# Linear attention and a SiLU layer on one core: second-product blocks between a batch's attention steps, a merged kv product, and a new order of loads

## The chip, the cores and the metric

The kernel runs on 1 core of one Trainium2 chip. The metric is the device time of one execution in microseconds. A profile is one further execution, recorded instruction by instruction; its span runs from the first to the last instruction, and its own time is a little longer than the span. The engines are TensorE (PE, its weight loads PEld), VectorE (DVE), ScalarE (ACT), GpSimd (POOL), and SyncE (SP), which only issues transfers.

## What is computed

Batch 8, 8 heads, 576 positions, 64 channels per head; the layer behind it maps 512 to 2048 to 512. Weights and data arrive and leave in float32.

```python
q_s = exp(q - max(q, -1)); q_s /= sum(q_s, -1)        # over the channels of a head
k_s = exp(k - max(k, 2));  k_s /= sum(k_s, 2)         # over the positions
kv  = einsum('bhsd,bhse->bhde', k_s, v)
x   = einsum('bhsd,bhde->bhse', q_s, kv)              # then (4608 tokens, 512)
h   = x @ w_in                                        # first product, 512 -> 2048
out = (h * sigmoid(h)) @ w_out                        # second product, 2048 -> 512
```

## The kernel before

**Attention of a batch.** q, k and v come in two head groups (`cc` 0 and 1), each a tile of 128 partitions by 1152 numbers. ScalarE takes the exponentials (`exp_q` L105, `exp_k` L108). `qsum` (L115) sums q over its channels on VectorE and takes the reciprocal, `qnorm` (L122) multiplies by it, mostly on GpSimd. The normalised q is transposed to `qT`: on TensorE for the first two batches (`tr` L140, copied from PSUM by `trcopy` L149), by a transposing DMA for the others (`q_transpose` L134). `vcast` (L110) casts v into `vaug`, which has a column of constants behind each head, so that `kv` (L153) gives the sum for k's normalisation along with the product. `kv` accumulates in PSUM banks 6 and 7; `kvcopy` (L165) divides by that column and writes `kvn`. `xt_mm` (L186) then multiplies `kvn` and `qT`, and `xt_evac` (L196) casts the result to `XTS`, the transposed input of the layer; `xt` (L200) does both for a head group, always through banks 6 and 7.

**The layer.** The 4608 tokens go in chunks of 512 (`NCH` is 9). Chunk 0 is special: its first product is done for the whole batch 0, 576 tokens wide, in 16 "wide" units of 8 matmuls (`wide_mm` L217, `wide_silu` L228), which rotate through three pairs of banks, 0 to 5. Chunk 1 then has only its remaining 448 tokens to do (`mm1` L252, banks 0 and 1 in turn). A unit's h goes through a tanh on ScalarE (L212) and one multiply on VectorE (L213) into `GTS`. Chunk 0's second product is a plain one, 16 blocks of four matmuls over all 512 outputs (`mm2_plain` L267), which accumulate in banks 2 to 5; `mm2_plain_out` (L277) scales them into output tiles and stores them. From chunk 1 on the second product goes by Strassen's seven products (`prod` L316, two halves each), with differences of weights T1 to T4 (`t_op` L306; T3 is written into part of W2 itself) and of activations (`s_op` L296), all on VectorE.

**The order** is written out by hand. Each engine runs its instructions in the order in which the program emits them. After the start-up, which is listed line by line, a list `units` holds the blocks for TensorE: 16 wide units (0 to 15); then, from `b1 = begin[1]` = 16 on, 32 units with chunk 1's first product and chunk 0's plain second product in turn; then 30 units for each later chunk. `plan(u, f)` puts a step in front of unit `u`: all steps planned for `u` are emitted, in the order in which they were planned, and then the unit. The steps for batch 1 lie in front of the wide units, those for batch 2 among chunk 1's units, those for batch t + 1 in chunk t.

**Loads.** Batch 0 comes over SP's queue; W1 (`load_w1`, with a cast to bfloat16), W2 (`load_w2`, to float16) and batches 1 and 2 over GpSimd's queue, where an issue stands in line with GpSimd's computing; batches from 3 on over SP's. Each of the tiles `qt`, `kt` and `vt` has three buffers, one and a half batches. `heat` (L400) runs matmuls on a constant tile into bank 5.

Of the kernel before, what the change touches and what calls it, by code (L numbers as in the profile page):

```python
# [17 lines left out]
def kernel(  # L18
# [96 lines left out]
    def qsum(b, cc):  # L115
        if "zq" not in st[b]:
            st[b]["zq"] = ap.tile([128, 2, J, 2], FP32, name="zq", bufs=2)
            st[b]["rzq"] = ap.tile([128, 2, J, 2], FP32, name="rzq", bufs=2)
        nc.vector.reduce_sum(out=st[b]["zq"][:, cc], in_=half(st[b]["eq"], cc), axis=AX.X)  # L119
        nc.vector.reciprocal(out=st[b]["rzq"][:, cc], in_=st[b]["zq"][:, cc])  # L120
# [44 lines left out]
    def kvcopy(b, cc):  # L165
        kp = PS[:, 6:8, cc * 128:cc * 128 + E1]
        rz = ap.tile([128, 2], FP32, name="rz", bufs=2)
        nc.vector.reciprocal(out=rz, in_=kp[:, :, D])
        nc.vector.tensor_tensor(
            out=kvn[b % 3][:, cc],  # L170
            in0=kp[:, :, 0:D],
            in1=rz[:, :, None].to_broadcast([128, 2, D]),
            op=ALU.mult,
        )
# [102 lines left out]
    def mm2_plain_out(t):  # L277
        for i, m in enumerate((1, 2, 3, 0)):
            o = mp.tile([128, DM], FP32, name="op", bufs=2)
            if i % 2 == 0:  # L280
                nc.scalar.activation(out=o, in_=PS[:, 2 + m], func=ACT.Copy, scale=OS)
            else:
                nc.vector.tensor_scalar_mul(out=o, in0=PS[:, 2 + m], scalar1=OS)  # L283
# [132 lines left out]
    heat(18)  # L416
# [4 lines left out]
    vcast(0, 0, nc.gpsimd, 1, 2)  # L421
# [28 lines left out]
    trcopy(0, 1, 5, J, 3)  # L450
# [12 lines left out]
    wide_mm(1, (0, 1), (0,))  # L463
# [4 lines left out]
    wide_mm(1, (0, 1), (1,))  # L468
# [36 lines left out]
    def first(part):  # L505
        for n in range(2):
            if part == 0:
                mm1_mm(1, FB[n], n, (0, 1))
            else:
                mm1_mm(1, FB[n], n, (2, 3))  # L510
                mm1_silu(1, FB[n], n)
# [64 lines left out]
    plan(b1 + 10, lambda: t_op(2, nc.vector, 0, 4))
# [9 lines left out]
    for i, x in enumerate((29, 31)):  # L586
        plan(b1 + x, lambda i=i: xt(2, i))
# [63 lines left out]
```

## Time and profile before

| | |
|---|---|
| three runs | 294.33, 297.22, 297.41 us; median 297.22 |
| profiled execution | 296.02 us, span 294.2 us |
| mean granted TensorE clock | 0.98 |
| busy, PE / PEld / DVE / ACT / POOL | 268.8 / 169.9 / 200.9 / 156.6 / 71.1 us |
| moved by DMA | 45.85 MB, 156 GB/s over the span |

Line numbers (L213) are those of the kernel before. In rows of the order of time stand start, length, engine, line, operation, out<-in with shapes, number of instructions, and in square brackets how long the engine was idle just before and what released it. In rows of waits stand the waiting engine and line, what it waited for, the total in us, how often, and the longest. In rows of DMA issues stand the queue, the number, the size as it arrives, and the time from issue to landing. A busy PE is not a PE at its peak: the granted clock tells how fast it was let run.

### The profile page before, as it was taken

How to read it: one execution, taken by the hardware profiler on the slowest of the kernel's cores; microseconds unless marked ns; L12 is line 12 of the kernel's file. 1: busy time of each engine (PE TensorE's matmuls, PEld its weight loads, DVE VectorE, ACT ScalarE, POOL GpSimd, SP SyncE). 2: the span in 40 equal slices, each digit the busy share in tenths (PEclk: the TensorE clock that was granted, in tenths of full speed). 3: DMA queues.
4: the chain of work that ended last, by engine and by line, in shares of the span. 5: the costliest groups of instructions: out<-in, count | busy, mean ns of one | idle time of the engine just before them, and what ended most of it. 6: DMA issues, size and time to landing. Idle time of an engine off the chain costs nothing.

```text
span 294.2 us, 5752 instructions
## 1 busy us (share of the span) xinstructions
PE 268.8 (91%) x2339; PEld 169.9 (58%) x2372; DVE 200.9 (68%) x287; ACT 156.6 (53%) x236; POOL 71.1 (24%) x58
## 2 busy tenths in 40 slices
PE   8696969997699999999999999999999999999980
PEld 3354734443356666665665666566666666666860
DVE  3748554796299749975995699579947755775810
ACT  5747562563466468545856584667464446445120
POOL 1964832081018001800460064007200000000000
PEclk9999798999979999999999999999999999999998
DMA  7899999119877638664864678350324004200506
GB/s 256 262 250 274 311 234 376 59 40 331 264 204 196 237 74 240 166 230 106 276 166 165 145 238 244 101 125 14 68 48 98 2 0 88 57 0 18 128 0 143
DMA packets 36074, 45.85 MB, mean 156 GB/s; under 512 B 16080, under 2 KB 20688, under 8 KB 36048
## 3 DMA queue, kind: packets, MB, share of 16 engines
q1 hardware_dynamic: 29568, 34.22, 41.2%
q0 software_dynamic: 6480, 11.27, 15.2%
q8 instruction: 18, 0.29, 0.4%
q14 instruction: 8, 0.07, 0.1%
HBM read 36.70 MB, written 9.44 MB: 157 GB/s over the span
## 4 chain that ended last, share of the span: by engine, by line
PE 76%; DVE 11%; ACT 4%; DMA 3%; issue 2%; POOL 1%; SPq 1%; DVEq 0%; ACTq 0%; POOLq 0%
PE PS L240 33%; PE PS L328 31%; PE PS L220 4%; DVE GT L213 3%; DMA vt<-in_v_dram 3%; PE PS L269 2%; DVE S L304 2%; DVE zq L119 2%; PE PS L157 2%; PE PS L190 2%; ACT XT L86 1%; ACT sg L212 1%; DVE T L314 1%; DMA out_dram<-op 1%; PE PS L402 1%
## 5 line engine op out<-in xcount | busy, mean ns | idle before, releaser
L212 ACT ACTIVATE sg<-PS 128x512 f32<-128x512 f32 (+2 forms) x144 | 85.5, 598 | 99.5 <-PE PS L240 89.3
L213 DVE SCALAR_TENSOR_TENSOR GT<-sg,PS 128x512 f16<-128x512 f32 (+2 forms) x144 | 96.5, 679 | 61.0 <-ACT sg L212 60.5
L240 PE MATMUL PS<-XT,W 128*128 128x512 bf16 (+1 forms) x480 | 126.3, 381 | 5.1 <-DVE op L283 3.2
L240 PEld LDWEIGHTS <-W 128*128 128x128 bf16 x512 | 49.5, 99 | 43.7 <-issue 6.2
L125 POOL TENSOR_TENSOR eq<-eq,rzq 128x1152 bf16<-128x1152 bf16 x15 | 31.6, 2116 | 126.5 <-ACT sg L212 83.1
L328 PEld LDWEIGHTS <-S 128*128 128x128 f16 x512 | 49.6, 98 | 18.4 <-issue 2.1
L328 PEld LDWEIGHTS <-GT 128*128 128x128 f16 x384 | 37.5, 99 | 14.6 <-issue 2.6
L328 PE MATMUL PS<-W,S 128*128 128x256 f16 x256 | 32.9, 273 | 0.8 <-ACT sb L344 0.7
L328 PE MATMUL PS<-W,GT 128*128 128x256 f16 x256 | 33.3, 276 | 0.1
L328 PE MATMUL PS<-T,S 128*128 128x256 f16 x256 | 32.7, 273 | 0.0
L304 DVE TENSOR_TENSOR S<-GT 128x2048 f16<-128x2048 f16 x16 | 25.2, 1574 | 0.0
L119 DVE TENSOR_REDUCE zq<-eq 128x18 f32<-128x1152 bf16 x16 | 21.5, 1345 | 4.2 <-ACT eq L105 4.2
L88 POOL CAST vaug<-vt 128x1152 bf16<-128x1152 f32 (+1 forms) x15 | 22.7, 1536 | 0.8 <-DMA vt<-in_v_dram 0.8
L105 ACT ACTIVATE eq<-qt 128x1152 bf16<-128x1152 f32 x16 | 18.6, 1162 | 2.4 <-DMA qt<-in_q_dram 2.4
L108 ACT ACTIVATE ek<-kt 128x1152 bf16<-128x1152 f32 x16 | 18.6, 1163 | 1.4 <-DMA kt<-in_k_dram 1.4
L220 PE MATMUL PS<-XT,W 128*128 128x288 bf16 x128 | 18.5, 299 | 0.6 <-ACT XT L86 0.3
L86 ACT CAST XT<-PS 128x1024 bf16<-128x1024 f32 (+2 forms) x17 | 16.4, 964 | 5.0 <-PE PS L190 5.0
L328 PE MATMUL PS<-T,GT 128*128 128x256 f16 x128 | 16.5, 273 | 0.7 <-ACT sc L344 0.7
L269 PE MATMUL PS<-W,GT 128*128 128x512 f16 x64 | 16.3, 379 | 0.0
L220 PEld LDWEIGHTS <-W 128*128 128x128 bf16 x128 | 12.7, 102 | 5.4 <-issue 1.0
L304 DVE TENSOR_TENSOR S<-GT,S 128x2048 f16<-128x2048 f16 x8 | 13.7, 1718 | 0.0
L402 PE MATMUL PS<-warm 128*128 128x512 bf16 x31 | 9.6, 466 | 2.0 <-DVE warm L387 1.2
(48 smaller groups left out, 138.6 us busy)
## 6 DMA issues: line engine op xcount, KB each, us to landing
out_dram<-ow SPq DMA_DIRECT2D x64, 128.0 KB, 2.4
qt<-in_q_dram SPq DMA_DIRECT2D x12, 576.0 KB, 4.9
kt<-in_k_dram SPq DMA_DIRECT2D x12, 576.0 KB, 6.4
vt<-in_v_dram SPq DMA_DIRECT2D x12, 576.0 KB, 7.5
qt<-in_q_dram POOLq DMA_DIRECT2D x4, 576.0 KB, 8.7
kt<-in_k_dram POOLq DMA_DIRECT2D x4, 576.0 KB, 9.4
vt<-in_v_dram POOLq DMA_DIRECT2D x4, 576.0 KB, 11.6
W<-in_moe_w_out_dram POOLq DMA_DIRECT2D x4, 512.0 KB, 14.1
```

Of the source, the lines that this page charges most:

```text
L86: eng.copy(out=o, in_=i)
L88: eng.tensor_copy(o, i)
L105: nc.scalar.activation(out=half(st[b]["eq"], cc), in_=jgd(b, "qt", cc), func=ACT.Exp)
L119: nc.vector.reduce_sum(out=st[b]["zq"][:, cc], in_=half(st[b]["eq"], cc), axis=AX.X)
L125: eng.tensor_tensor(out=e, in0=e, in1=r[:, :, :, None].to_broadcast([128, J, 2, D]), op=ALU.mult)
L212: nc.scalar.activation(out=s, in_=i, func=ACT.Tanh, scale=OS)
L213: nc.vector.scalar_tensor_tensor(out=o, in0=s, scalar=1.0, in1=i, op0=ALU.add, op1=ALU.mult)
L220: nc.tensor.matmul(out=PS[:, 2 * (fb % 3) + n, 0:S // 2], lhsT=W1[:, c, fb * 128:(fb + 1) * 128], rhs=XTS[0][:, c, n * (S // 2):(n + 1) * ...
L240: nc.tensor.matmul(out=PS[:, bank, o0:TCH], lhsT=W1[:, c, fb * 128:(fb + 1) * 128], rhs=XTS[t % 2][:, c, o0:TCH], start=(c == 0), stop=(c ...
L269: nc.tensor.matmul(out=PS[:, 2 + tb, :], lhsT=GTS[t % 2][:, fc, tb * 128:(tb + 1) * 128], rhs=W2[:, fc, :], start=(fc == 0), stop=(fc == N ...
L304: eng.tensor_tensor(out=SS[i - 1], in0=in0, in1=in1, op=op)
L328: nc.tensor.matmul(out=PS[:, WBANK[i], m * HN:(m + 1) * HN], lhsT=a[:, fc, m * 128:(m + 1) * 128], rhs=bb[:, fc, :], start=(first and m == ...
```

## The change

- Chunk 1's 32 units are reordered. Before, two units of its first product came first, then two blocks of the second, then the two in turn, with batch 1's last kv and X products all ahead of the first unit. Now four blocks of chunk 0's second product come first, batch 1's cast of v, kv products and the two X products are planned in front of the second, third and fourth of them, and three units of chunk 1's first product are left for the end.
- `kv_both` runs the kv products of both head groups and one `kvcopy`; it takes the place of two separate steps for batches 1 to 7 (batch 0 keeps two).
- `qsum` can do one head of a group at a time, so that the two halves are planned in front of different units (batches 1 and 2).
- `mm2_plain_out` writes into the wide tiles `ow` (three buffers, shared with the later chunks) in place of its own tile `op` (two buffers).
- In the start-up, GpSimd no longer casts v before it issues W1; ScalarE does; the second head group's casts of v and kv product are moved ahead of the first matmuls with W1, and the warming matmuls change in number and once in bank.
- W2's first quarter is issued ahead of batch 1's v; the other parts, and batch 2's loads, at other places of GpSimd's order; batch 3's loads four units earlier.
- The steps of batches 1 and 2 and the T differences are planned in front of other units.

```diff
-    def qsum(b, cc):
+    def qsum(b, cc, gs=None):
...
+        z, e = st[b]["zq"][:, cc], half(st[b]["eq"], cc)
+        if gs is None:
+            nc.vector.reduce_sum(out=z, in_=e, axis=AX.X)
+        else:
+            nc.vector.reduce_sum(out=z[:, :, gs], in_=e[:, :, gs, :], axis=AX.X)
+        if gs != 0:
+            nc.vector.reciprocal(out=st[b]["rzq"][:, cc], in_=z)
...
-    def kvcopy(b, cc):
...
+    def kvcopy(b, c0=0, c1=2):
+        kp = PS[:, 6:8, 0:256].rearrange("p r (c x) -> p r c x", x=128)[:, :, c0:c1, 0:E1]
+        rz = ap.tile([128, 2, 2], FP32, name="rz", bufs=2)[:, :, 0:c1 - c0]
+        nc.vector.reciprocal(out=rz, in_=kp[:, :, :, D])
+        for c in range(c0, c1):
+            nc.vector.tensor_tensor(
+                out=kvn[b % 3][:, c],
...
+    def kv_both(b):
+        kv(b, 0)
+        kv(b, 1)
+        kvcopy(b)
...
     def mm2_plain_out(t):
-        for i, m in enumerate((1, 2, 3, 0)):
-            o = mp.tile([128, DM], FP32, name="op", bufs=2)
...
+        for ms in ((1, 2), (3, 0)):
+            ow = mp.tile([128, 2, DM], FP32, name="ow", bufs=3)
+            for i, m in enumerate(ms):
+                if i == 0:
+                    nc.scalar.activation(out=ow[:, i], in_=PS[:, 2 + m], func=ACT.Copy, scale=OS)
+                else:
+                    nc.vector.tensor_scalar_mul(out=ow[:, i], in0=PS[:, 2 + m], scalar1=OS)
+                store(t, m * 128, ow[:, i])
...
-    heat(18)
+    heat(22)
...
     qnorm(0, 0, nc.gpsimd)
-    vcast(0, 0, nc.gpsimd, 1, 2)
     load_w1(0, 2)
...
     load(1, "kt", k, 1, nc.gpsimd)
+    load_w2(0, 4)
     load(1, "vt", v, 0, nc.gpsimd)
     load(1, "vt", v, 1, nc.gpsimd)
-    load_w2(0, 4)
-    load_w2(4, 8)
...
-    vcast(0, 0, nc.scalar, 0, 1)
+    vcast(0, 0, nc.scalar)
...
-    trcopy(0, 0, 0, 5, 0, nc.scalar)
+    trcopy(0, 0, 0, 5, 0)
...
-    heat(4)
+    heat(3)
...
     xt_mm(0, 0, 320, 256, 0, 0)
+    trcopy(0, 1, 5, J, 3)
+    vcast(0, 1, nc.scalar, 0, 1)
+    vcast(0, 1, nc.vector, 1, 2)
     xt_evac(0, 0, 4, 0, 320, 0, nc.scalar)
     xt_evac(0, 0, 0, 0, 256, 320, nc.vector)
-    vcast(0, 1, nc.scalar, 0, 1)
-    vcast(0, 1, nc.vector, 1, 2)
+    heat(4, 6)
+    kv(0, 1)
+    kvcopy(0, 1, 2)
     trcopy(0, 1, 0, 5, 2, nc.scalar)
-    heat(8)
     wide_mm(0, (0, 1))
-    kv(0, 1)
-    kvcopy(0, 1)
-    wide_mm(1, (0, 1), (0,))
     xt_mm(0, 1, 0, 320, 6, 0)
...
-    wide_mm(1, (0, 1), (1,))
+    wide_mm(1, (0, 1))
...
-    units += [lambda: first(0), lambda: first(1), lambda: mm2_plain(0, 0), lambda: mm2_plain(0, 1)]
-    for i in range(2, NFB):
-        units += [a1[i], lambda i=i: mm2_plain(0, i)]
+    units += [lambda i=i: mm2_plain(0, i) for i in range(4)] + a1[:1]
+    for i in range(4, NFB):
+        units += [a1[i - 3], lambda i=i: mm2_plain(0, i)]
+    units += a1[NFB - 3:]
...
-    plan(5, lambda: exp_q(1, 0))
-    plan(6, lambda: (qsum(1, 0), qnorm(1, 0, nc.gpsimd)))
-    plan(7, lambda: (load_w2(8, 12), exp_q(1, 1)))
-    plan(8, lambda: (qsum(1, 1), qnorm(1, 1, nc.gpsimd)))
-    plan(9, lambda: (load_w2(12, 16), load(2, "qt", q, 0, nc.gpsimd)))
-    plan(9, lambda: (tr(1, 0, 0, 5, 6), tr(1, 0, 5, J, 7)))
...
-    plan(14, lambda: vcast(1, 0, nc.gpsimd))
-    plan(15, lambda: (kv(1, 0), kvcopy(1, 0)))
-    plan(b1, lambda: (vcast(1, 1, nc.gpsimd, 0, 1), vcast(1, 1, nc.scalar, 1, 2)))
-    plan(b1, lambda: (kv(1, 1), kvcopy(1, 1)))
-    plan(b1, lambda: (xt(1, 0), xt(1, 1, nc.vector)))
...
+    plan(6, lambda: exp_q(1, 0))
+    plan(7, lambda: qsum(1, 0, 0))
+    plan(8, lambda: (qsum(1, 0, 1), qnorm(1, 0, nc.gpsimd)))
+    plan(8, lambda: (load_w2(4, 8), exp_q(1, 1)))
+    plan(9, lambda: qsum(1, 1, 0))
+    plan(10, lambda: (qsum(1, 1, 1), qnorm(1, 1, nc.gpsimd)))
+    plan(10, lambda: (load_w2(8, 12), load_w2(12, 16)))
+    plan(11, lambda: exp_k(1, 0))
+    plan(11, lambda: (tr(1, 0, 0, 5, 6), tr(1, 0, 5, J, 7)))
...
+    plan(13, lambda: (tr(1, 1, 0, 5, 6), tr(1, 1, 5, J, 7)))
...
+    plan(14, lambda: exp_k(1, 1))
+    plan(14, lambda: (load(2, "qt", q, 0, nc.gpsimd), load(2, "qt", q, 1, nc.gpsimd)))
+    plan(14, lambda: (vcast(1, 0, nc.gpsimd), load(2, "kt", k, 0, nc.gpsimd)))
+    plan(b1 + 1, lambda: (vcast(1, 1, nc.gpsimd, 0, 1), vcast(1, 1, nc.scalar, 1, 2)))
+    plan(b1 + 1, lambda: kv_both(1))
+    plan(b1 + 1, lambda: (load(2, "kt", k, 1, nc.gpsimd), load(2, "vt", v, 0, nc.gpsimd)))
...
+    plan(b1 + 2, lambda: xt(1, 0))
+    plan(b1 + 3, lambda: xt(1, 1))
...
-    plan(b1 + 5, lambda: t_op(1, nc.vector, 0, 4))
-    plan(b1 + 6, lambda: t_op(1, nc.vector, 4, 8))
+    plan(b1 + 8, lambda: t_op(1, nc.vector, 0, 4))
+    plan(b1 + 10, lambda: t_op(1, nc.vector, 4, 8))
...
-    plan(b1 + 10, lambda: t_op(2, nc.vector, 0, 4))
-    plan(b1 + 12, lambda: t_op(2, nc.vector, 4, 8))
-    plan(b1 + 20, lambda: t_op(4, nc.vector, 0, 4))
...
+    plan(b1 + 17, lambda: q_transpose(2))
+    plan(b1 + 19, lambda: t_op(2, nc.vector, 0, 4))
+    plan(b1 + 20, lambda: t_op(2, nc.vector, 4, 8))
+    plan(b1 + 22, lambda: t_op(4, nc.vector, 0, 4))
+    plan(b1 + 23, lambda: t_op(4, nc.vector, 4, 8))
+    plan(b1 + 25, lambda: t_op(3, nc.vector, 0, 4))
+    plan(b1 + 26, lambda: t_op(3, nc.vector, 4, 8))
-    for i, x in enumerate((21, 23)):
+    for i, x in enumerate((20, 21)):
         plan(b1 + x, lambda i=i: vcast(2, i, nc.gpsimd))
-        plan(b1 + x + 3, lambda i=i: (kv(2, i), kvcopy(2, i)))
-    plan(b1 + 28, lambda: loads(3, nc.sync))
-    for i, x in enumerate((29, 31)):
+    plan(b1 + 24, lambda: kv_both(2))
+    plan(b1 + 24, lambda: loads(3, nc.sync))
+    for i, x in enumerate((27, 30)):
         plan(b1 + x, lambda i=i: xt(2, i))
...
-            for i, x in enumerate((19, 21)):
-                pl(x, lambda i=i, b=b: (kv(b, i), kvcopy(b, i)))
+            pl(20, lambda b=b: kv_both(b))
```

More of the change, by code (lines that the diff above doesn't have):

```diff
@@ L118, in qsum @@
             st[b]["rzq"] = ap.tile([128, 2, J, 2], FP32, name="rzq", bufs=2)
-        nc.vector.reduce_sum(out=st[b]["zq"][:, cc], in_=half(st[b]["eq"], cc), axis=AX.X)
-        nc.vector.reciprocal(out=st[b]["rzq"][:, cc], in_=st[b]["zq"][:, cc])
+        z, e = st[b]["zq"][:, cc], half(st[b]["eq"], cc)
[5 more added lines that the diff above has]
+            nc.vector.reciprocal(out=st[b]["rzq"][:, cc], in_=z)
     def qnorm(b, cc, eng):
@@ L163, in kv @@
                     )
-    def kvcopy(b, cc):
[L166 to L174, printed above, removed]
+    def kvcopy(b, c0=0, c1=2):
[5 more added lines that the diff above has]
+                out=kvn[b % 3][:, c],
+                in0=kp[:, :, c - c0, 0:D],
+                in1=rz[:, :, c - c0, None].to_broadcast([128, 2, D]),
+                op=ALU.mult,
+            )
+    def kv_both(b):
+        kv(b, 0)
+        kv(b, 1)
+        kvcopy(b)
     def pieces(t):
@@ L398, with heat @@
     nc.vector.memset(vaug[:, :, :, D:E1], 1.0 / XS)
-    def heat(n):
+    def heat(n, bank=5):
         for _ in range(n):
-            nc.tensor.matmul(out=PS[:, 5, :], lhsT=warm[:, 0:128], rhs=warm, start=True, stop=True)
+            nc.tensor.matmul(out=PS[:, bank, :], lhsT=warm[:, 0:128], rhs=warm, start=True, stop=True)
     def load_w1(f0, f1):
@@ L449 @@
     exp_k(0, 1)
-    trcopy(0, 1, 5, J, 3)
     heat(2)
@@ L503 @@
     a1 = a_units(1)
[L505 to L511, printed above, removed]
-    units += [lambda: first(0), lambda: first(1), lambda: mm2_plain(0, 0), lambda: mm2_plain(0, 1)]
-    for i in range(2, NFB):
-        units += [a1[i], lambda i=i: mm2_plain(0, i)]
+    units += [lambda i=i: mm2_plain(0, i) for i in range(4)] + a1[:1]
+    for i in range(4, NFB):
+        units += [a1[i - 3], lambda i=i: mm2_plain(0, i)]
+    units += a1[NFB - 3:]
     for t in range(2, NCH):
@@ L572 @@
+    plan(b1 + 2, lambda: xt(1, 0))
+    plan(b1 + 3, lambda: xt(1, 1))
+    plan(b1 + 8, lambda: t_op(1, nc.vector, 0, 4))
+    plan(b1 + 10, lambda: t_op(1, nc.vector, 4, 8))
+    for i, x in enumerate((12, 14)):
         plan(b1 + x, lambda i=i: exp_q(2, i))
-        plan(b1 + x + 1, lambda i=i: (qsum(2, i), qnorm(2, i, nc.gpsimd)))
+        plan(b1 + x + 1, lambda i=i: qsum(2, i, 0))
+        plan(b1 + x + 2, lambda i=i: (qsum(2, i, 1), qnorm(2, i, nc.gpsimd)))
         plan(b1 + x + 4, lambda i=i: exp_k(2, i))
-    plan(b1 + 18, lambda: q_transpose(2))
```

25 lines of the change are left out of this document (5 added, 20 removed).

## The prediction

> **What bounds the kernel now.** I read the page first, then the table of stages, the waits, and the order of time up to 84 us. TensorE is nearly always busy, and its clock is lowered at three places.
>
> ```profile
> span 294.2 us, 5752 instructions
> PE 268.8 (91%) x2339; PEld 169.9 (58%) x2372; DVE 200.9 (68%) x287; ACT 156.6 (53%) x236; POOL 71.1 (24%) x58
> PEclk9999798999979999999999999999999999999998
> ```
>
> So what can be won is TensorE's idle time and its slow stretches. The stage table (stage, length, PE, PEld, DVE, ACT, POOL busy, granted clock, DMA share, GB/s) has the slow ones, and ahead of the second a stretch in which TensorE is busy 1.60 of 4.33 us:
>
> ```profile
> 30.70:34.10 3.40, 3.40 (x20) 2.26 (x18) 1.20 (x3) 2.03 (x3) 3.40 (x4) 0.64 1.07 353
> ...
> 39.80:44.13 4.33, 1.60 (x45) 0.74 (x44) 1.90 (x6) 2.14 (x3) 2.75 (x4) 0.91 1.21 252
> 44.13:47.70 3.57, 3.57 (x16) 1.57 (x13) 1.56 (x2) 1.03 (x2) 1.77 (x3) 0.63 0.98 333
> ...
> 81.30:84.70 3.40, 3.37 (x13) 1.79 (x13) 3.14 (x5) 1.46 (x2) 0.00 (x0) 0.55 0.68 145
> ```
>
> A stretch of 3.4 us with the clock at 0.55 to 0.64 does some 1.7 us of work less (the edges of my stages are not quite the stretch's, and the rest of it is at half clock); that is my price for each, an estimate. The remaining 200 us run at full clock in equal chunks, as two starts of a chunk's first product in the chain that ended last show (108.33 and 136.43, 28.1 us apart). The first Strassen chunk begins at 75.34 in the order of time and so takes 33.0: about 5.0 are lost in it.
>
> ```profile
> 75.34 1.90 PE L240 MATMUL PS<-XT,W 128*128 128x512 bf16 x7
> ```
>
> ```profile
> 108.33 1.74 PE PS L240 x8
> ...
> 136.43 1.73 PE PS L240 x8
> ```
>
> **The change, part by part.** All is worked out against the profiled execution: 296.0 us, of which 294.2 are the span and 1.8 lie around it. It is 1.2 below the median 297.2 of the three runs.
>
> *Start-up.* Today GpSimd, after the normalisation that lets the transposes go at 9.45, casts half of v before it issues W1; and the batch's second kv product comes at 16.08, 1.5 us after its last input (the cast that ends at 14.56), because it stands on TensorE behind warming matmuls and the first ones with W1:
>
> ```profile
> 9.45 0.68 PE L143 MATMUL PS<-ident,eq 128*128 128x128 bf16 x9 [1.91 <-POOL eq L125]
> ...
> 9.72 1.43 POOL L88 CAST vaug<-vt 128x576 bf16<-128x576 f32 x1 [0.33 <-DMA vt<-in_v_dram]
> 11.09 2.41 POOL L405 DMA_DIRECT2D W<-in_moe_w_in_dram  x3
> 11.12 1.16 ACT L108 ACTIVATE ek<-kt 128x1152 bf16<-128x1152 f32 x1 [0.17 <-DMA kt<-in_k_dram]
> ...
> 13.82 0.74 DVE L88 CAST vaug<-vt 128x576 bf16<-128x576 f32 x1
> ...
> 16.08 0.48 PE L157 MATMUL PS<-vaug,ek 64*64 64x65 bf16 x36
> ...
> 17.20 0.44 PE L190 MATMUL PS<-qT,kvn 64*64 64x320 bf16 x8 [0.28 <-DVE kvn L169]
> ...
> 17.75 0.69 DVE L88 CAST XT<-PS 128x512 bf16<-128x512 f32 x1 [0.61 <-PE PS L190]
> ...
> 18.32 7.30 PE L220 MATMUL PS<-XT,W 128*128 128x288 bf16 x56 [0.33 <-ACT XT L86]
> ```
>
> Without the cast W1 goes out at about 9.45, 1.6 us earlier, into the time in which v's last half still lands. These are the issue of that half on SP's queue, its time to landing, and the packets of GpSimd's queue between 12 and 13 us, the first microsecond in which there are any:
>
> ```profile
> 3.35 0.48 SPq L94 DMA_DIRECT2D vt<-in_v_dram  x1
> ```
>
> ```profile
> vt<-in_v_dram SPq DMA_DIRECT2D x1, 576.0 KB, 9.2
> ```
>
> ```profile
> q0 software_dynamic: 25, 0.01, 23.8%
> ```
>
> So v lands near 12.6, and W1, issued at 11.09, moves nothing until 12.8 or so, 1.8 us later (25 packets in that microsecond). After the change it moves from about 11.3, and 1.3 us of v's landing are shared. The delay of v lies between 0 and those 1.3; I take 0.7, half, because each queue has work throughout. The Trainium skill ("DMA: Bandwidth & Descriptors", section "Queues, rings and completion order") says that an engine takes turns between queues packet by packet, which speaks against an earlier W1; no trace here shows the two together, and by it the delay would be near its upper end and the term near 0.9.
>
> Then, with the casts of v now ahead of XT's evacuation: v at 13.3, cast of 0.74 to 14.1, XT's evacuation of 0.69 to 14.8, on ScalarE a copy of qT of about that size to 15.5 (kv, 0.48, and its division on VectorE are done before), the X product of 0.44, an evacuation of 0.69, and the stream of W1 products starts at 16.8 instead of 18.32. Gain **1.5** (0.9 to 2.2). ScalarE's undivided cast of the first v, at the 1.16 of an exponential of its shape from 9.72 on, ends by 10.9, ahead of the exponential at 11.12, which waits for k; the four warming matmuls added at the start lie in the 1.91 us of idleness before 9.45. Both cost nothing; if k came earlier, the cast would cost the difference, 0.2.
>
> *Stage of 16 wide units.* One unit is 8 matmuls of 7.30/56, 1.04 us. The wait in it is for batch 1's transposes:
>
> ```profile
> 23.26 1.16 ACT L105 ACTIVATE eq<-qt 128x1152 bf16<-128x1152 f32 x1
> 23.39 0.76 DVE L213 SCALAR_TENSOR_TENSOR GT<-sg,PS 128x576 f16<-128x576 f32 x1 [0.23 <-ACT sg L212]
> ...
> 25.66 1.34 DVE L119 TENSOR_REDUCE zq<-eq 128x18 f32<-128x1152 bf16 x1
> ...
> 27.45 2.11 POOL L125 TENSOR_TENSOR eq<-eq,rzq 128x1152 bf16<-128x1152 bf16 x1 [3.25 <-DVE rzq L120]
> ...
> 29.62 1.08 PE L143 MATMUL PS<-ident,eq 128*128 128x128 bf16 x9 [2.69 <-POOL eq L125]
> ...
> 38.68 1.15 PE L220 MATMUL PS<-XT,W 128*128 128x288 bf16 x8
> ```
>
> The exponential moves one unit later, the transposes two. But the sum is cut in two with one unit's 0.75 multiply between. Counted from the stream's start S (18.32 today, when the exponential ends at S+6.1): exponential done S+7.2, the next unit's tanh and multiply S+8.5, half of the 1.34 sum S+9.2, the multiply between S+9.9, the other half and the reciprocal S+10.9, 2.11 of normalisation S+13.2. TensorE, which waits 0.3 twice for a bank whose multiply stands behind a half sum, has done unit 10 at S+11.0 and waits 2.2, not 2.7. I take it that this shorter wait no longer lowers the clock (rival one). Unit 15 then ends at S + 15.6 for what is left of 16 units + 1.4 for 18 transposes (0.68 for nine) + 3.0 of waits = S+20.0; before it was 39.83, S+21.5. Gain 1.5, of which 0.4 is only the kv product that moved out.
>
> *Blocks between attention steps.* Before, nothing lies between the two kv and two X products of batch 1, which is the idle stretch to 44.13; then come blocks of both products in pairs:
>
> ```profile
> 48.68 0.92 PE L240 MATMUL PS<-XT,W 128*128 128x448 bf16 x4
> ...
> 50.30 0.92 PE L240 MATMUL PS<-XT,W 128*128 128x448 bf16 x4
> ```
>
> A pair is 1.62 us, 0.75 for the first product's block and 0.87 for the second's. From 39.83 to 48.5 TensorE did two pairs, one kv and two X, 4.6 us; the other 4.1 are idle or slow clock. Afterwards four blocks of 0.87 stand there, so that kv's division and XT's casts are done beside them. What stays: the first block needs the banks of unit 14, whose tanh now stands behind the second exponential of k (0.85 by the same counting), and 0.5 at kv and at the one bank pair that both X products use. So 0.4 (kv moved in) is lost and 2.8 won, 2.4; with the 1.5 above, the stage and this give **3.9**.
>
> What covers it is on GpSimd: ahead of its cast for kv stand a normalisation of 2.1 and five issues (two of W2, three of batch 2), which the row below has at 0.77, then a cast of the first head group; by this it is done at S+21.7, when TensorE asks. Each us later is one us of TensorE. W2's first quarter, issued at 22.06 and landing in some 14.1, would come at 36.2; it is issued two loads earlier now, and wanted at S+20.0, 36.8.
>
> ```profile
> 22.06 0.77 POOL L411 DMA_DIRECT2D W<-in_moe_w_out_dram  x1 [0.46 <-DMA qt<-in_q_dram]
> ```
>
> ```profile
> W<-in_moe_w_out_dram POOLq DMA_DIRECT2D x4, 512.0 KB, 14.1
> ```
>
> *Rest of that chunk.* From 48.7 to 75.34 are 26.7 us; 14 pairs of 1.62 and 1.8 for kv and X of batch 2 make 24.5, so 2.2 are lost. The rows that bear on it, first two of the order of time, then two waits:
>
> ```profile
> 53.99 0.69 DVE L314 TENSOR_TENSOR T<-W,T 128x1024 f16<-128x1024 f16 x1
> ...
> 62.42 1.94 DVE L314 TENSOR_TENSOR T<-W,T 128x1024 f16<-128x1024 f16 x1
> ```
>
> ```profile
> PE PS L157 <- DVE kvn L169: 1.5, 1, 1.5
> ...
> PEld L157 <- DVE kvn L169: 1.0, 4, 0.3
> ```
>
> A T subtraction takes 0.69 alone and 1.94 beside GpSimd's work on batch 2. T2 moves down, into that work, and T3 and T4 follow it, each in two pieces: I count one at 1.94, three at 1.5, two at 0.69, 7.8 in all. kv of both head groups in one run drops the 1.5, its second half waiting for the first's division, but must have both of GpSimd's casts: by my counting it waits some 1.5 for them, and a block 0.5 for a bank. So 2.0 are lost, gain **0.2** (-1.5 to 2, the ends being no help from the merged run and no wait at all). The loads of batch 3 move four units up on SP, still behind the transpose there, and are wanted a chunk later: nothing.
>
> *Output of chunk 0.* Two waits, and the page's group of XT's casts:
>
> ```profile
> DVE op L283 <- DMA out_dram<-op: 4.5, 1, 4.5
> ...
> PE PS L240 <- DVE op L283: 3.2, 1, 3.2
> ```
>
> ```profile
> L86 ACT CAST XT<-PS 128x1024 bf16<-128x1024 f32 (+2 forms) x17 | 16.4, 964 | 5.0 <-PE PS L190 5.0
> ```
>
> Two output tiles for four evacuations: the third waits for a store, and TensorE for its bank. Two wide tiles of three hold all four, so this wait goes, with its 1.7 of slow clock: the 5.0 above. Late next is ScalarE: the last three units now come with no block between, and XT's cast of 0.96 stands ahead of the last two tanh, so that the next chunk's first units wait for a bank by about that, 1.0. Gain **4.0** (3 to 5). SP issues the same eight stores.
>
> *kv in the five later chunks.* 0.25 each by the row of four waits (1.0), **1.2** (0 to 2); one reciprocal fewer on VectorE is not on the path.
>
> Sum 1.5 + 3.9 + 0.2 + 4.0 + 1.2 = 10.8; 296.0 - 10.8 = 285.2, and with a part of the 1.2 by which the median stands higher **285.5**.
>
> **The rivals.** *One: the clock falls again.* A wait of 2.69 was enough for a slow stretch, and 2.2 with 0.6 just before it is near. Price 1.7: 287.2. For it speaks how near the waits are; against, that the 1.91 us of idleness ahead of 9.45 lowered nothing. The Trainium skill ("TensorE: Matmul & The Clock Gate", section "Why this matters for your kernels") asks only for no gaps over about 3 us; the trace's 2.69 disagrees, and by the rule this rival would have no chance.
>
> *Two: VectorE holds the second half of chunk 1 up.* If all six late T pieces take 1.94, not the 7.8 in all that I counted, it lags 3.8 more; then 289.3. For it: the 1.94. Against: GpSimd's casts end before T3.
>
> *Three: slower, by GpSimd's queue.* Each issue can wait for an earlier transfer, and kv of batch 1 stands behind all:
>
> ```profile
> POOL vt L94 <- DMA W<-in_moe_w_in_dram: 2.1, 1, 2.1
> ```
>
> Six issues (three of W2, three of batch 2) precede that cast. At 2.1 each it is 12.6 late, and two slow stretches add 3.4: 285.5 + 16 = 301.5. From 10.8 late on the gain is eaten, from 14 the kernel is slower by more than 1%. For it: that wait is for a transfer issued long before, and W2 now stands ahead of v. Against: the issues come later than today's, with fewer transfers in flight, and one such wait is all the trace has.
>
> *Four: the blocks don't fill the gap*, because they wait for unit 14's banks or W2 themselves: 2.4 lost, 288.
>
> **How the numbers follow.** The forecast (282 to 287) 0.50, rival one 0.17, two 0.10, four 0.08, three 0.05; better than all, the transposes' wait gone, 279 to 282, 0.05; several terms failing at once, about 294, 0.05. The low ends of the terms, with one slow stretch, add to 4.6 (291.4), the high ones, with 5.5 for the stage and its blocks when the transposes' wait goes, to 16.7 (279.3). The range 281 to 292 leaves out about 2 in 10. Three runs spread over 294.33 to 297.41, so 1% is about what can be told from no change: faster by more 0.90, within it 0.05 (the several failing), slower 0.05.
>
> **What would show it.** Right: W1's stream starting near 16.8; blocks of the second product between kv and X products; no wait on a store by the output copies; the first Strassen chunk at 28 to 29 us; one or no slow stretch before 85. Wrong: kv of batch 1 waiting for a GpSimd cast, v landing past 14, or VectorE late in the T pieces.

## The result, and the profile after

The changed kernel takes 283.31 us (median of four runs, 283.05 to 283.58); the kernel before takes 296.88 (294.33 to 297.41). The ratio is 0.956, with a 95% interval of 0.950 to 0.962: 13.6 us less; 285.5 had been foretold, 11.4 less than the kernel before. Runs in which the chip was disturbed are left out of all comparisons here.

Line numbers have moved: the first product is L251 (L240 before), the plain second product L280 (L269), the wide units L231 (L220), the multiply L224 (L213), kv L162 (L157), the X product L201 (L190), Strassen's products L339 (L328), the T differences L325 (L314). The page after:

```profile
span 281.8 us, 5748 instructions
PE 263.9 (94%) x2342; PEld 167.9 (60%) x2371; DVE 199.1 (71%) x284; ACT 157.5 (56%) x236; POOL 69.6 (25%) x57
...
PEclk9999999999999999999999999999999999999998
```

No slice before the last is slow any more. The table of stages for the three places that were slow (same columns as before; the first pair is the transposes' wait, then the blocks, then the output of chunk 0):

```profile
25.30:29.80 4.50, 3.12 (x25) 2.28 (x25) 4.47 (x8) 3.32 (x5) 2.17 (x2) 1.00 1.17 278
29.80:33.20 3.40, 3.14 (x35) 2.49 (x35) 2.35 (x6) 2.26 (x4) 3.36 (x3) 1.00 1.14 331
36.30:42.20 5.90, 5.13 (x97) 2.24 (x95) 2.09 (x5) 3.04 (x5) 4.77 (x7) 1.00 1.23 230
42.20:45.80 3.60, 3.60 (x20) 1.76 (x18) 1.24 (x2) 1.44 (x4) 0.00 (x0) 1.00 1.04 412
66.50:70.70 4.20, 3.57 (x20) 1.61 (x18) 2.85 (x5) 3.76 (x7) 0.00 (x0) 1.00 0.94 370
70.70:74.10 3.40, 3.40 (x25) 2.29 (x24) 3.40 (x6) 2.06 (x3) 0.00 (x0) 1.00 0.70 167
```

Where TensorE was busy 1.60 of 4.33 us it is now busy 5.13 of 5.90, and the clock stays at 1.00. The order of time up to the first Strassen chunk, TensorE's rows that answer to those of before, and one of ScalarE's:

```profile
12.63 0.68 ACT L86 CAST vaug<-vt 128x576 bf16<-128x576 f32 x1 [0.26 <-DMA vt<-in_v_dram]
...
15.30 4.13 PE L231 MATMUL PS<-XT,W 128*128 128x288 bf16 x28
...
19.98 4.09 PE L231 MATMUL PS<-XT,W 128*128 128x288 bf16 x32 [0.54 <-DMA W<-in_moe_w_in_dram]
...
25.32 3.11 PE L231 MATMUL PS<-XT,W 128*128 128x288 bf16 x24 [1.25 <-DMA W<-in_moe_w_in_dram]
...
29.79 0.68 PE L148 MATMUL PS<-ident,eq 128*128 128x128 bf16 x9 [1.35 <-POOL eq L130]
...
33.20 3.10 PE L231 MATMUL PS<-XT,W 128*128 128x288 bf16 x24
...
37.46 0.59 PE L280 MATMUL PS<-W,GT 128*128 128x512 f16 x2 [0.73 <-DVE GT L224]
...
37.98 0.81 PE L162 MATMUL PS<-vaug,ek 64*64 64x65 bf16 x72
...
38.72 1.04 PE L280 MATMUL PS<-W,GT 128*128 128x512 f16 x4
...
39.69 0.38 PE L201 MATMUL PS<-qT,kvn 64*64 64x448 bf16 x4
...
40.00 1.04 PE L280 MATMUL PS<-W,GT 128*128 128x512 f16 x4
...
41.08 0.38 PE L201 MATMUL PS<-qT,kvn 64*64 64x448 bf16 x4
41.40 1.04 PE L280 MATMUL PS<-W,GT 128*128 128x512 f16 x4
...
42.27 1.68 PE L251 MATMUL PS<-XT,W 128*128 128x448 bf16 x8
```

The group at 15.30 holds four early matmuls of unit 1; the stream itself starts near 16.1. From there the reader sees two waits for W1 (0.54 and 1.25) that the prediction did not have, one for the normalisation (1.35), one for unit 14's bank (0.73), and then kv, block, X, block, X, block with no wait in between. The rest of the chunk, and two starts of a chunk in the chain that ended last:

```profile
55.27 2.41 DVE L325 TENSOR_TENSOR T<-W,T 128x1024 f16<-128x1024 f16 x1
...
58.27 0.92 PE L251 MATMUL PS<-XT,W 128*128 128x448 bf16 x4 [0.50 <-DVE GT L224]
...
60.31 0.48 PE L162 MATMUL PS<-vaug,ek 64*64 64x65 bf16 x36 [0.72 <-POOL vaug L88]
...
68.91 1.89 PE L251 MATMUL PS<-XT,W 128*128 128x512 bf16 x7 [0.43 <-DVE GT L224]
```

```profile
96.85 1.73 PE PS L251 x8
124.63 1.73 PE PS L251 x8
```

The first Strassen chunk runs from 68.91 to 96.85, 27.9 us instead of 33.0; the next takes 27.8 instead of 28.1. So at the stream's start the kernel is 2.2 us ahead, at the first Strassen chunk 6.4 (75.34 to 68.91), at the second 11.5 (108.33 to 96.85), at the end 12.4 (294.2 to 281.8).

### The profile page after: what moved, and what is told of

It reads as the page before. It is cut to its first block, busy times and chain, and to the rows that moved or that the text cites. A ratio compares the mean times of both kernels' runs of the same rounds, so it can differ in the third digit from the quotient of the medians.

```text
span 281.8 us, 5748 instructions
## 1 busy us (share of the span) xinstructions
PE 263.9 (94%) x2342; PEld 167.9 (60%) x2371; DVE 199.1 (71%) x284; ACT 157.5 (56%) x236; POOL 69.6 (25%) x57
## 4 chain that ended last, share of the span: by engine, by line
PE 80%; DMA 5%; POOL 4%; DVE 3%; issue 3%; ACT 3%; POOLq 0%; ACTq 0%; DVEq 0%
PE PS L251 36%; PE PS L339 36%; DMA W<-in_moe_w_in_dram 4%; PE PS L280 3%; POOL eq L130 3%; PE PS L201 2%; PE PS L162 2%; DMA qt<-in_q_dram 1%; DVE GT L224 1%; POOL vaug L88 1%; PE PS L231 1%; ACT eq L105 1%; DVE zq L123 1%; ACT sg L223 1%; DVE zq L121 0%
## 5 line engine op out<-in xcount | busy, mean ns | idle before, releaser
L224 DVE SCALAR_TENSOR_TENSOR GT<-sg,PS 128x512 f16<-128x512 f32 (+2 forms) x144 | 96.8, 679 | 58.4 <-ACT sg L223 58.1
L251 PE MATMUL PS<-XT,W 128*128 128x512 bf16 (+1 forms) x484 | 124.5, 375 | 2.4 <-DVE GT L224 0.9
L251 PEld LDWEIGHTS <-W 128*128 128x128 bf16 x512 | 49.9, 98 | 40.2 <-issue 2.3
L339 PEld LDWEIGHTS <-S 128*128 128x128 f16 x512 | 49.2, 98 | 17.4 <-issue 2.1
L339 PEld LDWEIGHTS <-GT 128*128 128x128 f16 x384 | 37.1, 98 | 13.9 <-issue 2.1
L339 PE MATMUL PS<-W,S 128*128 128x256 f16 x256 | 33.0, 273 | 0.8 <-ACT sb L355 0.7
L339 PE MATMUL PS<-W,GT 128*128 128x256 f16 x256 | 32.7, 273 | 0.1
L339 PE MATMUL PS<-T,S 128*128 128x256 f16 x256 | 32.7, 273 | 0.0
L88 POOL CAST vaug<-vt 128x1152 bf16<-128x1152 f32 (+1 forms) x14 | 21.3, 1547 | 0.0
L86 ACT CAST XT<-PS 128x1024 bf16<-128x1024 f32 (+2 forms) x18 | 17.3, 960 | 4.4 <-PE PS L201 3.7
L231 PE MATMUL PS<-XT,W 128*128 128x288 bf16 x128 | 17.1, 286 | 1.9 <-DMA W<-in_moe_w_in_dram 1.8
L121 DVE TENSOR_REDUCE zq<-eq 128x18 f32<-128x1152 bf16 x12 | 16.1, 1345 | 3.7 <-ACT eq L105 3.7
L280 PE MATMUL PS<-W,GT 128*128 128x512 f16 x64 | 16.6, 380 | 0.7 <-DVE GT L224 0.7
L339 PE MATMUL PS<-T,GT 128*128 128x256 f16 x128 | 16.5, 273 | 0.7 <-ACT sc L355 0.7
L231 PEld LDWEIGHTS <-W 128*128 128x128 bf16 x128 | 12.1, 98 | 6.1 <-DMA W<-in_moe_w_in_dram 2.4
```

Of the source, the lines that this page charges most:

```text
L86: eng.copy(out=o, in_=i)
L88: eng.tensor_copy(o, i)
L224: nc.vector.scalar_tensor_tensor(out=o, in0=s, scalar=1.0, in1=i, op0=ALU.add, op1=ALU.mult)
L231: nc.tensor.matmul(out=PS[:, 2 * (fb % 3) + n, 0:S // 2], lhsT=W1[:, c, fb * 128:(fb + 1) * 128], rhs=XTS[0][:, c, n * (S // 2):(n + 1) * ...
L251: nc.tensor.matmul(out=PS[:, bank, o0:TCH], lhsT=W1[:, c, fb * 128:(fb + 1) * 128], rhs=XTS[t % 2][:, c, o0:TCH], start=(c == 0), stop=(c ...
L280: nc.tensor.matmul(out=PS[:, 2 + tb, :], lhsT=GTS[t % 2][:, fc, tb * 128:(tb + 1) * 128], rhs=W2[:, fc, :], start=(fc == 0), stop=(fc == N ...
```

## The experiments

Four of them undo one part of the changed kernel each: the output tiles, the order of the blocks, kv by head group and the start-up. Differences are taken against the 283.31 of the changed kernel unless another time is named. The runs were made on three chips. The kernel before took 296.65, 295.8 and 295.84 us on them, so that a few tenths between runs of different chips tell nothing.

**The output tiles.** `mm2_plain_out` as before, with two tiles `op`.

```diff
-        for ms in ((1, 2), (3, 0)):
-            ow = mp.tile([128, 2, DM], FP32, name="ow", bufs=3)
+        for i, m in enumerate((1, 2, 3, 0)):
+            o = mp.tile([128, DM], FP32, name="op", bufs=2)
...
```

> The changed kernel with chunk 0's output back in its own two tiles. Theory of the sum (the wait for a store and the slow stretch behind it make the whole term): 4.0 to 5.1 us more than the changed kernel, 287.3 to 288.4, with one slow clock stretch of 3.4 us back. Rival (only the wait counts, the clock stays): 3.2 us more, 286.5, no slow stretch. Rival (the evacuation was late anyway behind three tanh): under 2 us more.

Measured 287.99 (287.54 to 288.78), 4.7 more. The waits and the stage table of this kernel:

```profile
DVE op L294 <- DMA out_dram<-op: 3.6, 1, 3.6
...
PE PS L251 <- DVE op L294: 3.0, 1, 3.0
```

```profile
71.90:75.00 3.10, 0.15 (x3) 0.03 (x1) 0.78 (x2) 1.58 (x3) 0.00 (x0) 1.00 0.62 136
76.50:79.90 3.40, 3.40 (x16) 1.87 (x14) 3.40 (x4) 2.46 (x5) 0.00 (x0) 0.54 0.55 139
```

TensorE does almost nothing for 3.1 us, and 1.5 us later runs 3.4 us at about half clock: 3.0 of waiting, and 1.7 by the prediction's price for such a stretch, add to the 4.7. The 1.7 is an estimate; a trial of it follows below.

**The same tiles without the other parts.** The kernel before, with only `mm2_plain_out` replaced.

```diff
-            o = mp.tile([128, DM], FP32, name="op", bufs=2)
+            ow = mp.tile([128, 2, DM], FP32, name="ow", bufs=3)
...
```

> The kernel before, with the new output tiles alone. Theory (this part is worth the same without the others, 4.7): 4.2 to 5.2 less than the kernel before. Rival (the last blocks of the old order keep ScalarE or VectorE late enough that TensorE waits for the bank anyway): under 3.5 less.

Measured 291.06 (290.67 to 291.27), 4.8 less than the 295.84 of the kernel before beside it. By the medians the part is worth the same with and without the others. The profile shows that the other stages do not stand still meanwhile: no slow stretch is left at the output, but none is behind the transposes' wait either (the clock is 1.00 from 29.73 to 38.14), and the one behind the gap of batch 1's products is twice as long as in the kernel before:

```profile
29.59 0.68 PE L143 MATMUL PS<-ident,eq 128*128 128x128 bf16 x9 [1.75 <-POOL eq L125]
```

```profile
40.63:47.46 6.83, 5.83 (x21) 2.09 (x21) 2.33 (x3) 1.99 (x3) 3.56 (x6) 0.50 1.13 337
77.50:81.00 3.50, 3.50 (x27) 2.37 (x25) 3.50 (x5) 2.38 (x4) 0.00 (x0) 1.00 0.73 163
```

So one slow stretch less and one more cancel in this profile.

**The order of the blocks.** Chunk 1's units in the old order, and batch 1's last cast of v, kv and X products ahead of all of them; kv stays merged, and the rest of batch 1's steps stay where the change put them.

```diff
-    units += [lambda i=i: mm2_plain(0, i) for i in range(4)] + a1[:1]
+    units += [lambda: first(0), lambda: first(1), lambda: mm2_plain(0, 0), lambda: mm2_plain(0, 1)]
...
-    plan(b1 + 1, lambda: kv_both(1))
+    plan(b1, lambda: kv_both(1))
+    plan(b1, lambda: (xt(1, 0), xt(1, 1, nc.vector)))
```

> The changed kernel with chunk 1's units in the old order: two units of the first product ahead, and batch 1's kv (still merged) and both X products ahead of them with nothing between. Theory of the sum: the 2.4 us of the blocks come back, less some 0.4 because three units in a row no longer stand at the end: 1.5 to 3 us more, 284.8 to 286.3, with a slow clock stretch behind the gap. Rival (the gap was mostly the separate kv products, not the missing blocks): under 1 us more.

Measured 287.64 (286.51 to 289.51): 4.3 more, above the expectation, and with a spread of 3.0 where the changed kernel has 0.5. The gap and the stretch behind it:

```profile
36.20:41.20 5.00, 2.03 (x82) 1.29 (x82) 2.28 (x6) 2.18 (x4) 4.61 (x7) 0.98 1.24 206
41.20:44.60 3.40, 3.40 (x11) 1.31 (x10) 1.55 (x3) 1.09 (x2) 0.00 (x0) 0.53 1.09 380
```

**What of that is the clock.** The kernel with the old order, with warming matmuls (their results are not used) in the waits ahead of kv and X; the waits themselves stay.

```diff
-    plan(b1, lambda: kv_both(1))
-    plan(b1, lambda: (xt(1, 0), xt(1, 1, nc.vector)))
+    plan(b1, lambda: (heat(2, 3), kv(1, 0), heat(3, 3), kv(1, 1), kvcopy(1)))
+    plan(b1, lambda: (heat(3, 3), xt(1, 0), heat(4, 3), xt(1, 1, nc.vector)))
```

> The kernel with the old order of blocks, with 2, 3, 3 and 4 warming matmuls into a free bank in the four waits ahead of batch 1's kv and X products (0.48, 0.83, 0.82 and 1.00 us); the waits stay. Theory (the slow stretch behind the gap is worth 1.7 of the 4.3 that the old order costs): 1.2 to 2.2 less than its 287.6, 285.4 to 286.4, and a narrower spread. Rival (the clock is a by-product): 287 or more.

Measured 285.3 (285.13 to 286.1): 2.3 less than without them, and a spread of 1.0. The same two stretches:

```profile
36.20:41.20 5.00, 4.55 (x92) 2.39 (x94) 2.46 (x6) 1.98 (x3) 4.41 (x7) 1.00 1.24 209
41.20:44.60 3.40, 3.00 (x15) 1.36 (x14) 1.86 (x3) 0.98 (x2) 0.00 (x0) 1.00 1.08 386
```

The clock stays at 1.00 although not one useful matmul was added, so the slow stretch comes from TensorE's idle time and goes away when that time is filled, usefully or not. By the medians 2.3 of the 4.3 that the old order costs are the clock, but these two kernels ran on different chips. The two traces, each of a run near the low end, give less: the first Strassen chunk starts at 71.83 with the old order, at 70.52 with the warming matmuls and at 68.91 in the changed kernel, which is 1.3 for the one slow stretch and 1.6 for the waits. The other three runs of the old order had a lower clock still (0.969 to 0.981, for 0.985 in the profiled one); no trace shows where they lost it.

**The same trial on the output's wait.** The kernel with the old output tiles, with 12 warming matmuls into a free bank ahead of the unit that waits.

```diff
+    plan(begin[2] + 3, lambda: heat(12, 7))
```

> The kernel with the old output tiles, with 12 warming matmuls into a free PSUM bank put where TensorE waits for the bank of the store-bound tile (2.95 us); the wait itself stays. Theory (a wait of 3 us costs itself plus 1.7 for the slow stretch behind it): 1.7 us less than the 288.0 of that kernel, 286.3, and no slow stretch in the chunk's first half. Rival (the 4.7 are the wait and what VectorE and ScalarE have to catch up, the clock is a by-product): 288.0 or more.

Measured 288.06 (287.85 to 289.82), no less than without. The stage behind the wait, and the wait:

```profile
75.80:79.90 4.10, 4.10 (x28) 2.62 (x28) 4.10 (x6) 3.06 (x5) 0.00 (x0) 1.00 0.88 207
```

```profile
DVE op L294 <- DMA out_dram<-op: 4.8, 1, 4.8
```

The slow stretch is gone, as the theory has it, but VectorE waited 4.8 us for the store instead of 3.6: one of the stores' issues on SP took 1.8 us. Why the issue was longer with the matmuls beside it wasn't found, so this run neither confirms nor refutes the price of 1.7 in this place.

**kv by head group.** For batches 2 to 7; batch 1 stays merged.

```diff
-    plan(b1 + 24, lambda: kv_both(2))
+    for i, x in enumerate((24, 26)):
+        plan(b1 + x, lambda i=i: (kv(2, i), kvcopy(2, i, i + 1)))
...
-            pl(20, lambda b=b: kv_both(b))
+            for i, x in enumerate((19, 21)):
+                pl(x, lambda i=i, b=b: (kv(b, i), kvcopy(b, i, i + 1)))
```

> The changed kernel with kv and its division by head group again for batches 2 to 7 (batch 1 stays merged). Theory of the sum: 0.25 per chunk, and up to 1.5 at batch 2: 0.9 to 2.2 us more, 284.2 to 285.5, with TensorE waiting for the first division at each second kv. Rival (the merged run waits for both casts of GpSimd at batch 2 as long as the split one for the division): 0.9 to 1.1 from the later chunks alone, nothing at batch 2.

Measured 286.63, 3.3 more and above the expectation, in two groups: 285.03 and 285.38 at a granted clock of 0.996 to 0.997, 287.88 and 288.15 at 0.985. In the profiled execution (the first of them) the second kv of batch 2 waits for the first's division, and chunks are 28.0 us apart instead of 27.8:

```profile
61.73 0.48 PE L162 MATMUL PS<-vaug,ek 64*64 64x65 bf16 x36 [1.17 <-DVE kvn L175]
```

```profile
97.50 1.73 PE PS L251 x8
...
125.48 1.73 PE PS L251 x8
```

That is 0.65 at batch 2 (97.50 for 96.85) and 0.2 in each later chunk, 1.7 in all; the two shorter runs are 1.7 and 2.1 above the changed kernel, as the theory had it. The other two are 2.9 longer at the lower clock; no profile of such a run was taken, so that the waits at batch 2 let the clock fall in them is argued, not shown.

**The start-up.** The old list of start-up lines.

```diff
-    heat(22)
+    heat(18)
...
+    vcast(0, 0, nc.gpsimd, 1, 2)
     load_w1(0, 2)
...
-    kv(0, 1)
-    kvcopy(0, 1, 2)
     trcopy(0, 1, 0, 5, 2, nc.scalar)
+    heat(8)
     wide_mm(0, (0, 1))
+    kv(0, 1)
+    kvcopy(0, 1, 2)
```

> The changed kernel with the old start-up: GpSimd casts half of the first v before it issues W1, the second kv stands behind the first matmuls with W1. Theory of the sum: the stream of W1 products starts 2.2 us later and the end moves by 1.5 to 2.2: 284.8 to 285.5. Rival (W1's third and fourth pieces land at nearly the same time in both kernels, at 19.9 and 25.3 for 20.3 and 25.7, and TensorE now waits 0.5 and 1.3 for them): most of the earlier start is given back there, and undoing it costs 0.3 to 0.9: 283.6 to 284.2.

Measured 285.29 (285.25 to 285.4), 2.0 more. The rival falls: unit 8 of this kernel waits for W1 too, and starts 1.5 later than in the changed one, at 26.84 for 25.32:

```profile
26.84 3.11 PE L231 MATMUL PS<-XT,W 128*128 128x288 bf16 x24 [1.18 <-DMA W<-in_moe_w_in_dram]
```

**Which half of the start-up.** Only GpSimd's cast ahead of W1 is put back; TensorE's order stays.

```diff
     qnorm(0, 0, nc.gpsimd)
+    vcast(0, 0, nc.gpsimd, 1, 2)
     load_w1(0, 2)
...
-    vcast(0, 0, nc.scalar)
+    vcast(0, 0, nc.scalar, 0, 1)
```

> The changed kernel, but GpSimd casts half of the first v again before it issues W1; TensorE's new start-up order stays. Theory (the 2.0 that undoing the whole start-up costs come from W1 being issued 1.8 us earlier, because everything behind waits for W1's later pieces): 1.0 to 2.0 more than the changed kernel, 284.3 to 285.3, with W1 pieces landing later by as much. Rival (they come from kv standing ahead of the first W1 matmuls): under 0.5 more.

Measured 284.56 (284.31 to 285.18), 1.3 more: some two thirds of the start-up's 2.0 are the cast that no longer stands ahead of W1 on GpSimd. The changed kernel was not run on this chip; the trace of the kernel with T1 and T2 earlier (below), made on it with the changed start-up, has unit 8 at 24.68 for 26.13 here, 1.45 earlier, which agrees. TensorE now waits for the first piece as well:

```profile
15.73 0.66 PE L231 MATMUL PS<-XT,W 128*128 128x288 bf16 x4 [1.28 <-DMA W<-in_moe_w_in_dram]
...
26.13 3.11 PE L231 MATMUL PS<-XT,W 128*128 128x288 bf16 x24 [1.28 <-DMA W<-in_moe_w_in_dram]
```

**Two waits that are left.** First batch 1's exponentials and sums, one unit earlier:

```diff
-    plan(6, lambda: exp_q(1, 0))
-    plan(7, lambda: qsum(1, 0, 0))
-    plan(8, lambda: (qsum(1, 0, 1), qnorm(1, 0, nc.gpsimd)))
+    plan(5, lambda: (exp_q(1, 0), qsum(1, 0, 0)))
+    plan(6, lambda: (qsum(1, 0, 1), qnorm(1, 0, nc.gpsimd)))
```

> The changed kernel with batch 1's exponentials and sums one unit earlier in the wide stage, the transposes where they are. Theory (the transposes wait for the chain exponential, sums, normalisation, and nothing else): the wait of 1.35 gone, 0.3 to 0.8 at the second transposes instead, 0.6 to 1.0 us less: 282.3 to 282.7. Rival (W1's third quarter, landing at 25.3, binds the stage, and later waits give the rest back): within 0.3 of 283.3.

Measured 282.57 (281.93 to 283.15). The first transposes no longer wait; the second ones wait 0.34:

```profile
27.51 0.67 PE L148 MATMUL PS<-ident,eq 128*128 128x128 bf16 x9
...
30.47 0.68 PE L148 MATMUL PS<-ident,eq 128*128 128x128 bf16 x9 [0.34 <-POOL eq L130]
...
37.12 0.48 PE L162 MATMUL PS<-vaug,ek 64*64 64x65 bf16 x36 [0.86 <-POOL vaug L88]
```

Unit 8 still waits 1.24, for 1.25. The second half of batch 1's kv, which did not wait in the changed kernel, now waits 0.86 for GpSimd's cast, so that much of what was won is given back there. The time is 0.7 less than the changed kernel's 283.31, 0.5 less than its 283.05 in the last runs below: the lower end of the theory's 0.6 to 1.0, with one of the rival's later waits. Then T1 and T2, earlier:

```diff
...
-    plan(b1 + 19, lambda: t_op(2, nc.vector, 0, 4))
-    plan(b1 + 20, lambda: t_op(2, nc.vector, 4, 8))
+    plan(b1 + 10, lambda: t_op(2, nc.vector, 0, 4))
+    plan(b1 + 12, lambda: t_op(2, nc.vector, 4, 8))
```

> The changed kernel with T1 two units and T2 nine or eight units earlier, ahead of GpSimd's work on batch 2. Theory (the late T2 pieces at 2.41 and 1.10 us beside GpSimd hold VectorE up, and GpSimd's casts too): T2 pieces of 0.69, the wait of 0.50 for a multiply and part of the 0.72 for GpSimd's cast gone: 0.5 to 1.2 us less, 282.1 to 282.8. Rival (kv of batch 2 waits for GpSimd's casts whatever VectorE does): within 0.3 of 283.3.

Three runs, 282.61, 282.91 and 283.75: no difference that they can tell. The T2 pieces do take 0.7, but kv of batch 2 then waits longer for GpSimd's cast, 1.00 for 0.72:

```profile
59.26 0.48 PE L162 MATMUL PS<-vaug,ek 64*64 64x65 bf16 x36 [1.00 <-POOL vaug L88]
```

The trace is the rival's: GpSimd binds there, and a faster VectorE is mostly given back as a longer wait. Last the changed kernel again, and beside it on the same chip a version with both of these, one issue of batch 2's k moved behind batch 1's last cast on GpSimd, and half of batch 2's second cast given to ScalarE:

```diff
...
-    for i, x in enumerate((20, 21)):
-        plan(b1 + x, lambda i=i: vcast(2, i, nc.gpsimd))
+    plan(b1 + 20, lambda: vcast(2, 0, nc.gpsimd))
+    plan(b1 + 21, lambda: (vcast(2, 1, nc.gpsimd, 0, 1), vcast(2, 1, nc.scalar, 1, 2)))
...
```

> The changed kernel as it is, on the same chip as the three beside it: 283.3, within 0.5.

> The changed kernel with batch 1's exponentials and sums one unit earlier, T1 and T2 earlier, one issue for batch 2's k behind batch 1's last cast of v on GpSimd, and half of batch 2's second cast of v on ScalarE. Theory (the waits that are left in the first 70 us are waits for GpSimd and each is worth its length): 1.0 from the transposes, 0.3 from the T pieces, 0.7 at each of the two kv products: 280.5 to 281.5. Rival (each of these waits is replaced by the next one, W1's landing or ScalarE): 282.3 or more.

The changed kernel took 282.65 to 283.36 in five runs, median 283.05; the new version 281.48 (281.27 to 282.81), a ratio to the kernel before of 0.953 (0.949 to 0.957). By the medians it is 1.6 us shorter than the changed kernel, just inside the expectation's upper end. The two longest of its six runs, 282.61 and 282.81, had a lower clock, 0.988 for 0.993 to 0.996, and reach into the changed kernel's times. The profile is of one of these two, and it has its slow stretch in the start-up, which is the same code as in the changed kernel, behind a wait of 1.78 for the first transposes:

```profile
7.90:11.31 3.41, 1.41 (x21) 0.90 (x25) 3.34 (x5) 2.33 (x2) 3.41 (x4) 1.00 1.03 395
11.31:14.72 3.41, 3.19 (x55) 1.88 (x56) 1.85 (x6) 2.26 (x3) 3.41 (x6) 0.50 1.27 181
```

The prediction took the 1.91 of idleness at this place in the kernel before, which lowered nothing, as a sign that such a wait is safe. It is not always.

## Why the prediction was right

**Start-up, 1.5 foretold, 2.2 seen in the trace, 2.0 by undoing it.** The term that was mis-sized is the delay of v: 0.7 was taken, nothing came. v's cast starts at 12.63, as its landing at 12.6 before allowed. The estimate took v to be moving at full rate until it landed. It was not: in the microsecond from 11 to 12 SP's queue (q1) was half idle already in the kernel before (first fence), and in the changed one W1 (q0) meets only 33 packets of it there (second fence) and 8 between 11.6 and 12.3 (third):

```profile
q1 hardware_dynamic: 94, 0.18, 46.8%
```

```profile
q0 software_dynamic: 205, 0.10, 89.3%
q1 hardware_dynamic: 33, 0.06, 14.5%
```

```profile
q1 hardware_dynamic: 8, 0.02, 6.6%
```

The last microsecond of the load is a thin tail of packets, which W1 did not delay. For the same reason no run here tests the turn-taking of two full queues that was quoted against the earlier W1. What the prediction lacked is W1's own pieces: they land late enough that TensorE waits 1.8 in all for two of them.

**Stage and blocks, 3.9 foretold, 4.2 seen** (6.4 at the first Strassen chunk, less 2.2), 4.3 by undoing the blocks. Unit 15 ends at 36.3, 36.8 was foretold. The transposes' wait is 1.35, not 2.2: TensorE comes later to it, since it lost 1.8 to W1; 1.8 and 1.35 are 3.1 where 3.0 of waits were foretold, so the sum held while its parts did not, which is luck. GpSimd's cast for kv was foretold at S+21.7, 37.8 with the S that came about; its cast ends at 38.04 and kv's first half starts at 37.98, so the cover holds, just. Unit 14's bank cost 0.73 for 0.85.

The stage's own 1.5 (halved sums, later transposes) was not undone by itself, and one trace speaks against it. In the profile of the kernel before with the new output tiles the stage is the old one, without a slow stretch, and takes 19.9 us, from 18.28 to 38.14; in the changed kernel it takes 20.2, from 16.1 to 36.3, and in the kernel before 21.5. What the stage won against that last profile is thus about its slow stretch, which not every execution of the kernel before has. That the term came out is in part luck; the blocks' share rests on undoing them.

**Rest of the chunk, 0.2 foretold, 0.0 seen** (6.4 ahead at 42.27 for 48.68 as at 68.91 for 75.34). The waits are those named, 0.50 for a bank and 0.72 instead of 1.5 for GpSimd. That T2 is slow beside GpSimd was right (2.41), that it matters much was not: without it the wait for GpSimd grows from 0.72 to 1.00.

**Output, 4.0 foretold, 5.05 seen less 0.2 that are kv's; 4.7 and 4.8 by undoing it and by doing it alone.** The wait that was to come instead, 1.0 for banks behind three tanh, is 0.43. **Later kv, 1.2 foretold, 0.9 seen** from the second Strassen chunk on (11.5 to 12.4).

**The rivals.** The clock did not fall again in the profiled execution: no slow stretch is left before the end, and the times spread over 0.5 us where the kernel before spreads over 3. In these cases the busy share places it: 3.12 of 4.50 us was enough, 2.03 of 5.00 and 1.60 of 4.33 were not. The advice of the Trainium skill, no idle gaps over about 3 us (page "TensorE: Matmul & The Clock Gate", section "Why this matters for your kernels"), does not describe the old order of blocks, where the longest single wait ahead of the slow stretch was 1.00; the short waits add up. The share alone does not settle it. The slow stretches of the kernel before begin at 29.73, 43.38 and 80.92 us and last 3.41 each, and their starts lie 4 and 11 such lengths apart. In the 3.41 us ahead of a slow stretch TensorE was busy 0.61 to 1.41 us in six cases of these traces (the end of the kernel left aside) and 1.68 in a seventh, the gap of batch 1's products in the kernel before with the new tiles; yet with 1.61 in the old start-up and 1.67 at that same kernel's transposes the clock stayed at 1.00. Where a gap falls against these 3.41 us thus seems to count too; no run varied that alone. GpSimd's queue did wait for transfers, 2.9 at one issue of v, but ahead of its work on kv and without delaying it. VectorE held chunk 1 up by 0.50 at one bank, not by the 3.8 of the rival.

## What to carry to other kernels

A string of short waits can cost twice: itself (1.6 us here), and nearly as much again in the slow stretch behind it (1.3). Fill it with work that is ready anyway; if there is none, matmuls with unused results bought back 1.3 us by the traces and 2.3 by the medians. Look at how busy TensorE was over the 3.4 us ahead of a slow stretch, the length of one such stretch in these traces, and not only at the longest gap. And when the third output tile of a burst waits for a store, look at the buffers first: tiles for all four evacuations were worth 4.7 us of 283 for a few lines, as much as the new order of the blocks. A wait for GpSimd that is taken away on TensorE tends to come back at the next thing that GpSimd must do, as two trials showed.

## What was not expected of the hardware

- The spread of a kernel's times tells of its clock: 3.0 us with the old order of blocks, 1.0 with warming matmuls in the same waits, 0.5 and 0.7 in two sets of runs of the changed kernel. With kv split, one and the same kernel has runs of 285.0 and of 288.2, at granted clocks of 0.997 and 0.985.
- A load's last microsecond was a thin tail: of v's last half 33 packets came between 11 and 12 us and hardly any after, and it landed at 12.6. A second queue moved 205 packets in that microsecond without delaying it.
- Twelve matmuls into an unused bank went with a store issue of 1.8 us on SP and a wait 1.2 longer; the cause is open.
- Much the same wait had a slow stretch behind it in one of these kernels' profiles and none in another's: at the first transposes of the start-up (1.91 without, 1.78 with), and at batch 1's transposes (2.69 with, 1.75 behind another of 1.11 without).
